# Block-recurrent attention with an ELU feed-forward: the states' result stored by quarters, the last quarter on two queues

## The chip, the cores and the metric

The kernel runs on one core of a Trainium2 chip. The metric is the device time of one execution in microseconds (us). Times given for a kernel are medians of several executions; the profile is one execution of its own, with a span from its first to its last instruction that is a little shorter than the measured time.

The engines are called as the profile calls them: PE is TensorE (matmuls; PEld is its weight load), DVE is VectorE, ACT is ScalarE, POOL is GpSimd, SP is SyncE. SPq and ACTq are the instruction queues of SP and ACT, where DMAs are issued.

## The reference, cut to what matters

```python
# x: (8, 8, 512, 64), state: (8, 8, 32, 64), w_in: (512, 2048), w_out: (2048, 512), all float32
scores = scale * x @ state.T                 # tokens read the states
xread = softmax(scores) @ state
scores2 = scale * state @ x.T                # states read the tokens
sread = softmax(scores2) @ x
y = concat([xread, sread], axis=2)           # per batch 512 token rows and 32 state rows
y = y.transpose(0, 2, 1, 3).reshape(8 * 544, 512)
h = y @ w_in
g = where(h > 0, h, exp(min(h, 0)) - 1)      # ELU
out = g @ w_out                              # (4352, 512)
```

Each of the 8 batches has 544 rows in the output: 512 for its tokens and, behind them, 32 for its states.

## The kernel before, in words

The work goes batch by batch. The first batch (`first_batch`) also loads and converts the weights, in an order that a written plan sets out. Batches 1 to 7 (`batch`) each compute the feed-forward of their 512 token rows and, woven in between, the attention of the next batch. The state rows of all batches, 8 x 32 = 256 of them, are kept in `read` and are computed together at the very end, in `states()` (lines 685 to 694), which runs once after the last batch.

`states()` first makes the hidden layer for the 256 rows, 128 features at a time (`ffn1_state`, with ACT and DVE making the ELU into `g_all`). Then it multiplies by `w_out` with one object of the class `Strassen` (lines 438 to 518). This is a scheme of Strassen's kind: the 256 x 512 result is cut into two halves of rows, h = 0 and 1, and two halves of columns, q = 0 and 1, and comes out of seven products where plain blocks would need eight. One product is 16 weight loads and 16 matmuls of 128 x 256 (`product`); the products accumulate in two PSUM banks, and after each of them one quarter of the result is copied or added into the SBUF tile `o_sb`, of 128 partitions x 2 (h) x 512 columns. `sums` makes the sums of blocks that the products take.

`steps()` returns the seven products in the order in which they run. `copy(ps, h, q)` is an ACT copy into quarter (h, q); `add(ps, h, q)` is a DVE addition onto what stands there:

```python
def p1(): ...; self.copy(bank_a, 0, 0)     # n = 0
def p2(): ...; self.add(bank_b, 0, 0)      # n = 1, and a DVE update of a12
def p6(): ...; self.copy(bank_a, 1, 0)     # n = 2
def p7(): ...; self.copy(bank_b, 1, 1)     # n = 3
def p5(): ...; self.add(bank_a, 1, 1)      # n = 4
def p4(): ...; self.add(bank_b, 1, 0)      # n = 5
def p3(): ...; self.copy(bank_a, 0, 1)     # n = 6
return [p1, p2, p6, p7, p5, p4, p3]
```

In a batch (line 683) the tile goes out in one DMA (`store`). In `states()` each batch's 32 rows lie elsewhere in the output, so there are eight DMAs, all on SP's queue, after the last step. Batch b's rows are the 32 partitions from (b mod 4) x 32, in half b // 4 of the tile.

What sets the order: PE and SP keep the order of the program throughout. ACT, DVE and POOL keep it in the first batch only; from batch 1 on (lines 698 and 699) the framework orders their instructions. The framework also makes every wait between engines and DMAs, from what each instruction reads and writes. `g_all`, `o_sb` and the weights are each one tile of which instructions use slices. The sequence at the program's end, that waits for all DMAs and brings the engines together, stands under line 728 in the profile.

Nearly all instructions carry line 94 in the profile, that of a helper, so groups are told apart by the tiles that they write and read. `out_dram<-o_sb` is a store of the result.

Of the kernel before, what the change touches and what calls it, by code (L numbers as in the profile page):

```python
# [25 lines left out]
def kernel(  # L26
# [15 lines left out]
    B, H, S, D = x.shape  # L42
    NS = state.shape[2]
    DM, DF = moe_w_in.shape
    P = 128
# [5 lines left out]
    SB = S + NS  # L51
# [8 lines left out]
    out_b = out.rearrange("(b s) c -> b s c", b=B)  # L60
# [27 lines left out]
    class InOrder:  # L88
# [10 lines left out]
    tensor, sync, vector, scalar, gpsimd = (  # L99
        InOrder(e) for e in (nc.tensor, nc.sync, nc.vector, nc.scalar, nc.gpsimd)  # L100
    )
# [292 lines left out]
    def ffn1_state(fo):  # L394

        ps = bank(3 + (fo + 1) % 3)[:, : B * NS]
        for co in range(NP):
            matmul(
                ps,
                w_in[:, fo // 2, co, fo % 2 * P : (fo % 2 + 1) * P],  # L400
                st["xT"][:, co].rearrange("p b s -> p (b s)"),
                start=(co == 0),
                stop=(co == NP - 1),
            )
        elu(ps, fo)
# [279 lines left out]
    def states():  # L685
        for fo in range(FO):
            ffn1_state(fo)
        half = Strassen(0)
        half.sums()
        for f in half.steps():  # L690
            f()
        for b in range(B):
            c, i = divmod(b, P // NS)
            sync.dma_start(out=out_b[b, S:SB], in_=half.o_sb[i * NS : (i + 1) * NS, c])

    first_batch()
    load_x(2, [sync])
# [2 lines left out]
    for b in range(1, B):  # L700
        batch(b)
    states()


# [28 lines left out]
```

## Time and profile before

| What | Value |
|---|---|
| Time, median of three executions | 774.3 us (773.92 to 775.31) |
| Span of the profiled execution | 773.4 us |
| The same execution as measured | 775.13 us |
| Mean granted clock of TensorE | 0.994 |
| Stores `out_dram<-o_sb` of 512 KB (token rows) | 16, on SPq |
| Stores `out_dram<-o_sb` of 64 KB (state rows) | 8, on SPq |
| Start of the first and the last of these eight | 767.6 and 770.8 us |

A line of a timeline or of a group names the engine, the line, the operation, the tiles (written <- read), the shapes and the number of instructions; "128x256 f32" is partitions x elements. In brackets stands how long the engine was idle before, and what ended that. A DMA's issuing instruction is short; when its data has landed is told apart, as the time from issue to landing.

### The profile page before, as it was taken

To read this page: it belongs to the slowest core of one execution; us is meant where nothing else is said; L and a number is where in the kernel's file an instruction comes from. 1 tells how busy PE (TensorE), PEld (TensorE's weight loads), DVE (VectorE), ACT (ScalarE), POOL (GpSimd) and SP (SyncE) were. 2 spreads that over 40 slices of the span, in tenths; PEclk is the share of its full clock that TensorE was granted. 3 is DMA by queue.
4 is the path that set the end of the run, shared out by engine and by line. 5 is a ranking of instruction groups with operands and counts; after the bars stand their busy time and mean duration, and the time that the engine had idled before them with its cause. 6 is when DMAs were issued, how large, how long until landed. Compare 5 with 4: busy or idle time off the path is not lost.

```text
span 773.4 us, 9742 instructions
## 1 busy us (share of the span) xinstructions
PE 744.9 (96%) x4016; PEld 499.8 (65%) x4016; DVE 351.7 (45%) x590; ACT 315.5 (41%) x585; POOL 35.1 (5%) x38
## 2 busy tenths in 40 slices
PE   3599999999999999999999999999999999999996
PEld 1234444468845786478846885578647884688885
DVE  2999979473135611481047413571148114601230
ACT  4799874642056213641164304630264106400420
POOL 0200002002000200010000200020001100000000
PEclk9899999999999999999999999999999999999999
DMA  9555400700030003000030003000000000000001
GB/s 283 217 200 198 108 1 28 137 1 22 7 83 1 1 28 81 1 1 28 28 56 1 2 27 82 1 1 28 27 1 1 28 4 24 1 28 1 27 1 27
DMA packets 44844, 35.22 MB, mean 46 GB/s; under 512 B 36352, under 2 KB 36352, under 8 KB 44800
## 3 DMA queue, kind: packets, MB, share of 16 engines
q1 hardware_dynamic: 41632, 33.82, 15.1%
q10 hardware_dynamic: 3168, 0.79, 0.5%
q8 instruction: 31, 0.51, 0.3%
q14 instruction: 13, 0.11, 0.0%
HBM read 25.69 MB, written 8.91 MB: 45 GB/s over the span
## 4 chain that ended last, share of the span: by engine, by line
PE 95%; DVE 2%; DMA 1%; ACT 1%; issue 0%; ACTq 0%; DVEq 0%
PE ps L94 95%; DMA x_sb<-in_x_dram 1%; DVE w_in L94 1%; DMA s_sb<-in_state_dram 0%; ACT raw L94 0%; DVE total_t L94 0%; ACT xT L94 0%; DVE top L94 0%; ACT e_sb L94 0%; DVE aT L94 0%; DVE t_sb L94 0%; DVE top_t L94 0%; ACT w_in L94 0%; ACT m_sb L94 0%; DVE total L94 0%
## 5 line engine op out<-in xcount | busy, mean ns | idle before, releaser
L94 PE MATMUL ps<-w_out,g_all 128*128 128x256 f32 (+1 forms) x1088 | 273.7, 406 | 0.0
L94 PEld LDWEIGHTS ps<-w_out,g_all 128*128 128x128 f32 x1088 | 205.2, 190 | 58.5 <-issue 31.3
L94 PE MATMUL ps<-aT,m_sb 128*128 128x512 f32 x512 | 228.2, 600 | 4.3 <-DVE aT L94 3.3
L94 PEld LDWEIGHTS ps<-aT,m_sb 128*128 128x128 f32 x512 | 96.9, 192 | 126.7 <-issue 119.5
L94 DVE SCALAR_TENSOR_TENSOR g_all<-e_sb,ps 128x512 f32<-128x512 f32 (+1 forms) x144 | 94.6, 658 | 169.6 <-ACT e_sb L94 169.6
L94 ACT ACTIVATE e_sb<-ps 128x512 f32<-128x512 f32 (+1 forms) x144 | 82.4, 572 | 96.0 <-PE ps L94 78.3
L94 ACT COPY o_sb<-ps 128x256 f32<-128x256 f32 (+1 forms) x62 | 23.4, 378 | 237.1 <-PE ps L94 237.1
L94 DVE TENSOR_TENSOR o_sb<-o_sb,ps 128x256 f32<-128x256 f32 x45 | 19.0, 421 | 208.6 <-PE ps L94 206.1
L94 PE MATMUL ps<-t_w,s 128*128 128x256 f32 x480 | 109.2, 381 | 0.0
L94 PEld LDWEIGHTS ps<-t_w,s 128*128 128x128 f32 x480 | 90.6, 190 | 17.1 <-issue 5.0
L94 ACT ACTIVATE e_sb<-e_sb 128x512 f32<-128x512 f32 (+1 forms) x144 | 87.2, 606 | 4.5
L94 PE MATMUL ps<-t_w,g_all 128*128 128x256 f32 x240 | 54.3, 379 | 0.0
L94 PEld LDWEIGHTS ps<-t_w,g_all 128*128 128x128 f32 x240 | 45.1, 190 | 5.9
L94 ACT ACTIVATE raw<-raw 128x512 f32<-128x512 uint32 x64 | 43.6, 681 | 1.0
L94 POOL TENSOR_TENSOR t_sb<-t_sb,top_t 128x512 f32<-128x512 f32 x16 | 17.6, 1108 | 542.1 <-DVE top_t L94 542.1
L94 PE MATMUL ps<-w_in,kT 64*32 64x512 f32 (+1 forms) x576 | 33.6, 554 | 0.0
L94 PE MATMUL ps<-xT_state,w_in 128*128 128x256 f32 x128 | 27.8, 379 | 0.0
L94 PEld LDWEIGHTS ps<-xT_state,w_in 128*128 128x128 f32 x128 | 24.3, 190 | 3.3
L94 ACT COPY m_sb<-ps 128x512 f32<-128x512 f32 x24 | 13.6, 581 | 29.2 <-PE ps L94 29.2
L94 DVE COPY m_sb<-ps 128x512 f32<-128x512 f32 x40 | 25.5, 681 | 0.0
L94 PEld LDWEIGHTS ps<-w_in,kT 64*32 64x32 f32 x576 | 9.3, 107 | 23.3 <-issue 19.4
L94 ACT COPY xT<-ps 128x512 f32<-128x512 f32 x32 | 16.6, 596 | 5.3 <-PE ps L94 5.3
(54 smaller groups left out, 379.6 us busy)
## 6 DMA issues: line engine op xcount, KB each, us to landing
raw<-in_moe_w_in_dram SPq DMA_DIRECT2D x16, 512.0 KB, 5.5
raw<-in_moe_w_out_dram SPq DMA_DIRECT2D x16, 512.0 KB, 3.3
out_dram<-o_sb SPq DMA_DIRECT2D x16, 512.0 KB, 2.7
x_sb<-in_x_dram SPq DMA_DIRECT2D x30, 256.0 KB, 5.0
x_sb<-in_x_dram ACTq DMA_DIRECT2D x2, 256.0 KB, 6.1
out_dram<-o_sb SPq DMA_DIRECT2D x8, 64.0 KB, 1.7
s_sb<-in_state_dram ACTq DMA_DIRECT2D x4, 64.0 KB, 2.9
s_sb<-in_state_dram SPq DMA_DIRECT2D x4, 64.0 KB, 2.6
```

The lines of the kernel that those rows point to most:

```text
L94: ins = getattr(self.engine, name)(*args, **kw)
```

## The change

In `states()`, the loop over the eight batches behind the last step goes. In its place, four of the seven steps are followed by four DMAs each, one for each group of 32 partitions, that store the quarter which this step completes: after n = 1 quarter (0, 0), after n = 4 quarter (1, 1), after n = 5 quarter (1, 0), after n = 6 quarter (0, 1). Each DMA moves 32 rows x 256 columns, 32 KB in pieces of 1 KB, where it was 32 rows x 512 columns, 64 KB in pieces of 2 KB. There are 16 DMAs instead of 8, with the same bytes in total. Twelve are on SP's queue; of the last four, two are on SP's and two on ACT's, by turns.

```diff
@@ -687,11 +687,21 @@
             ffn1_state(fo)
         half = Strassen(0)
         half.sums()
-        for f in half.steps():
+        for n, f in enumerate(half.steps()):
             f()
-        for b in range(B):
-            c, i = divmod(b, P // NS)
-            sync.dma_start(out=out_b[b, S:SB], in_=half.o_sb[i * NS : (i + 1) * NS, c])
+            quarter = {1: (0, 0), 4: (1, 1), 5: (1, 0), 6: (0, 1)}.get(n)
+            if quarter is None:
+                continue
+            c, q = quarter
+            cols = slice(q * DM // 2, (q + 1) * DM // 2)
+            for i in range(P // NS):
+                engine = scalar if n == 6 and i % 2 else sync
+                engine.dma_start(
+                    out=out_b[c * P // NS + i, S:SB, cols],
+                    in_=half.o_sb[i * NS : (i + 1) * NS, c, cols],
+                )
```

Here `c` is the half of rows h and `P // NS` is 4.

## The prediction

> **What bounds the kernel now.** I read the engine shares and the chain of waits first. TensorE is busy for 96% of the span, and the chain that ends last is TensorE for 95%. So anything that does not lie on TensorE's time, or after its last matmul, is hidden.
>
> ```profile
> PE 744.9 (96%) x4016; PEld 499.8 (65%) x4016; DVE 351.7 (45%) x590; ACT 315.5 (41%) x585; POOL 35.1 (5%) x38
> ...
> PE 95%; DVE 2%; DMA 1%; ACT 1%; issue 0%; ACTq 0%; DVEq 0%
> ```
>
> The change touches only the last stage, so the next view is the timeline of its end: start, length, engine, operation.
>
> ```profile
> 749.74 3.62 PE L94 MATMUL ps<-t_w,s 128*128 128x256 f32 x16
> 749.99 0.42 DVE L94 TENSOR_TENSOR o_sb<-o_sb,ps 128x256 f32<-128x256 f32 x1 [2.02 <-issue]
> ...
> 760.37 0.42 DVE L94 TENSOR_TENSOR o_sb<-o_sb,ps 128x256 f32<-128x256 f32 x1 [8.82 <-PE ps L94]
> ...
> 763.75 0.42 DVE L94 TENSOR_TENSOR o_sb<-o_sb,ps 128x256 f32<-128x256 f32 x1 [2.96 <-PE ps L94]
> ...
> 767.20 0.37 ACT L94 COPY o_sb<-ps 128x256 f32<-128x256 f32 x1 [9.99 <-PE ps L94]
> 767.60 3.63 SPq L94 DMA_DIRECT2D out_dram<-o_sb  x8
> ```
>
> The four writes shown complete the four quarters of the result buffer: (0,0) at 749.99 + 0.42 = 750.41, (1,1) at 760.79, (1,0) at 764.17, (0,1) at 767.57. All eight stores start after the last one, though three quarters have been ready for 3 to 17 us. The same stretch by the result buffer `o_sb` gives issue times (length min/median/max, first and last start) and the time from issue to landing:
>
> ```profile
> L94 SPq DMA_DIRECT2D out_dram<-o_sb x8: 344/420/432, 767.6 to 770.8; - x8
> ...
> DMA to landing us min/median/max: 1.6/1.7/1.7
> ```
>
> The eight starts are (770.8 - 767.6) / 7 = 0.46 us apart; one landing takes 1.7 us, hardly more for the last than for the first. So the queue's issuing rate sets the end, not the bandwidth. The table of stretches confirms it; its columns are the stretch, its length, five engines' busy time, the TensorE clock, the DMA share and GB/s:
>
> ```profile
> 767.57:770.81 3.24, 0.00 (x0) 0.00 (x0) 0.00 (x0) 0.01 (x1) 0.00 (x0) 1.00 0.41 104
> 770.81:772.52 1.71, 0.00 (x0) 0.00 (x0) 0.00 (x0) 0.00 (x0) 0.00 (x0) 0.51 0.43 110
> 772.52:773.35 0.83, 0.00 (x0) 0.00 (x0) 0.00 (x0) 0.00 (x0) 0.00 (x0) 0.50 0.00 0
> ```
>
> The tail after the last copy is 3.24 us of issuing, 1.71 us for the last landing, 0.83 us of the program's end: 5.78 us in which no engine computes, at some 104 GB/s. By source line, the end (line 728) is seven semaphore steps of SP and short drains.
>
> **What the Trainium skill says.** (1) "DMA: Bandwidth & Descriptors", section "Issuing engines are not separate DMA queues": DMAs from SP and ACT run on the same 16 DMA engines, and a second issuer saves only the sequencer's issue time. Issue time is just what this tail consists of (3.24 of 5.78 us), and the share of 0.41 says the DMA engines have room. (2) Same page, "Anatomy of one DMA": about 2.0 us fixed, mostly the write's receipt, and bytes / 436 GB/s on top; given for GpSimd's path. The trace has 1.7 us for 64 KB on SP's queue, which I use. By the page's slope, an estimate, 32 KB less saves 0.08 us: halving a store doesn't halve its landing. (3) Same page, "Rules for kernel authors": below 64 KB a transfer is mostly overhead. The change makes 16 stores of 32 KB of 8 of 64 KB; what matters is where the overhead lies.
>
> **The change part by part.** *Three quarters stored early (12 stores on SP).* Each quarter's four stores take 4 x 0.46 = 1.84 us of SP's queue. (0,0) would be issued from 750.4 to 752.3, (1,1) from 760.8 to 762.6, (1,0) from 764.2 to 766.0. The nearest gap to the next quarter is 764.17 - 760.79 = 3.4 us, so SP is idle again before each, and 1.6 us before the last at 767.57. SP keeps program order and has nothing else left: batch 7 issues no loads, and its last whole-tile store (line 683) comes ahead of this stage. Last landing of (1,0): about 764.2 + 1.4 + 1.7 = 767.3. Cost 0, hidden beside TensorE's products.
>
> Could these transfers slow the products? I compared a stretch that holds a 512 KB store with one that doesn't:
>
> ```profile
> 715.50:718.50 3.00, 3.00 (x16) 2.64 (x15) 0.42 (x1) 1.07 (x3) 0.00 (x0) 1.00 0.43 175
> ...
> 752.00:755.00 3.00, 3.00 (x16) 2.64 (x15) 0.00 (x0) 0.37 (x1) 0.00 (x0) 1.00 0.00 0
> ```
>
> Sixteen matmuls in 3.00 us either way: 0.
>
> *The last quarter, four stores on two queues.* Two on SP, two on ACT. SP: starts at 767.60 and 768.06. ACT has issued no DMA since the start of the program, so its price comes from there, where both queues loaded the states together:
>
> ```profile
> L94 ACTq DMA_DIRECT2D s_sb<-in_state_dram x4: 421/470/477, 0.7 to 2.2; - x4
> L94 SPq DMA_DIRECT2D s_sb<-in_state_dram x4: 374/440/451, 0.7 to 2.1; - x4
> ```
>
> Over the same 1.5 us each queue issued four, so they issue beside one another, ACT at 0.47 us. ACT's first store waits for its own copy, ended 767.57. The nearest row for that wait is ACT's drain in the end code, which starts at 767.2 and lasts up to 401 ns, thus to 767.61: 0.04 us after the copy. Hence ACT's stores start at about 767.61 and 768.10. Behind them on ACT stand only the drains of the end code, which wait for SP's side anyway, so no work is held up by ACT's issuing.
>
> *Landing of the last one.* 768.10 + 1.7 = 769.80. From below: half the bytes, -0.08 us (the skill's slope). From above: at the start, eight loads in flight from both queues took 2.2 to 3.2 us, median 2.8, in 256-byte pieces from HBM; 1.1 us over the 1.7. Here two stores of 32 KB start together, the 64 KB per 0.46 us that SP alone moves now, in pieces of 1 KB. I take 1.7.
>
> *The end.* The same 0.83 us; twice as many stores, but they are long landed. Bounds: 0 to 0.1 us for some more semaphore steps of 28 ns.
>
> Sum: 769.80 + 0.83 = 770.63 against 773.35, a gain of 2.72 us, made up of the issuing that goes from 3.24 to 0.53 us. The three other runs give 773.92 to 775.31, median 774.3, that is 0.9 us above this span (the profiled execution itself was measured at 775.13). The same gain from the median gives 774.3 - 2.7 = 771.6 us, -0.35%. A measurement of this kernel tells about 0.2%, 1.55 us, from no change; the gain is 1.75 times that.
>
> **The rivals.** *A, the forecast:* 771.6 us; with 0.7 us for the scatter of the runs, 770.9 to 772.3. Chance 0.76.
>
> *B, the buffer is guarded as a whole:* each write of a quarter waits until earlier stores have landed. (1,1): fourth store at 760.8 + 1.4, landed 763.9, so the add at 763.75 moves by 0.15; then (1,0) lands at about 767.4, and the last copy moves from 767.20 to 767.4. Some 0.2 us lost: 771.8. Against it: `g_all`, one tile, is written and read slice by slice without TensorE waiting. Chance 0.06.
>
> *C, the second queue brings little:* either ACT's stores land as late as the states' loads did (2.8 us: 770.9 + 0.83, gain 1.6), or the two queues take turns at issuing (fourth start at 767.6 + 3 x 0.46 = 769.0, end 771.5, gain 1.8). For it: ACT's queue is long idle, and a store on it isn't in the trace. Against: the side-by-side issues above. 772.5 to 772.7. Chance 0.13.
>
> *D, slower:* stores on different queues to the same output are ordered, each waiting for the landing of the one before, as SP and ACT alternate. The place is the last quarter: three handovers at 1.7 us put the last issue at 767.6 + 5.1 = 772.7, its landing at 774.4, the end at 775.2, +1.9 us: 776.2. It decides against the change from 3.2 / 3 = 1.07 us per handover. For it: before, all stores share one queue, so that ordering between queues was never seen. Against: the eight stores of one tensor don't wait for each other there, and their rows are disjoint. Chance 0.05.
>
> **How the numbers follow.** Faster by over 0.2% (below 772.75): nearly all of A (0.74), B (0.06), half of C (0.07): 0.87. Within: the rest of A and of C, 0.08. Slower: D, 0.05. The range takes A with its scatter and 0.1 us for a shorter landing, and reaches over C: 770.7 to 773.0, leaving out D and the scatter beyond C.
>
> **What would show it.** The timeline should have four groups of four stores, starting at 750.4, 760.8, 764.2 and 767.6, the last as two on SPq and two on ACTq, with 1.6 to 1.7 us to landing; SP's last start at 768.1 instead of 770.8; the span about 770.6. TensorE's products must keep their step of 3.45 us (749.74, 753.19, 756.64). B shows as an idle time of DVE or ACT before `o_sb` that ends on a DMA, C as a landing of over 2.5 us or starts 0.46 us apart across both queues, D as ACT's or SP's queue waiting for `out_dram`. The forecast is wrong if the last copy ends later than 767.6 by anything but scatter, or if the end takes over 1 us.

## The result, and the profile after

The changed kernel takes 771.95 us (median of 6 executions, 771.51 to 773.09) where the kernel before takes 774.7 us (median of 6, 773.84 to 775.34). The ratio is 0.9968 with a 95% interval of 0.9955 to 0.9981. That is 2.5 us less by the ratio and 2.75 us less by the medians; the forecast was 2.7 us. The profiled execution of the changed kernel spans 770.2 us, against 773.4 us.

First the timeline of the changed kernel's end, for the same instructions as before:

```profile
749.58 0.42 DVE L94 TENSOR_TENSOR o_sb<-o_sb,ps 128x256 f32<-128x256 f32 x1 [2.02 <-issue]
...
750.02 17.94 SPq L94 DMA_DIRECT2D out_dram<-o_sb  x14
...
759.95 0.42 DVE L94 TENSOR_TENSOR o_sb<-o_sb,ps 128x256 f32<-128x256 f32 x1 [8.81 <-PE ps L94]
...
763.33 0.42 DVE L94 TENSOR_TENSOR o_sb<-o_sb,ps 128x256 f32<-128x256 f32 x1 [2.96 <-PE ps L94]
766.78 0.37 ACT L94 COPY o_sb<-ps 128x256 f32<-128x256 f32 x1 [9.99 <-PE ps L94]
767.19 0.85 ACTq L94 DMA_DIRECT2D out_dram<-o_sb  x2
```

The first store now starts at 750.02, as soon as the first quarter is complete, and of the four that follow the last copy two are on ACT's queue. (The view merges SP's 14 stores into one line. Narrower timelines at 760.40 and 763.78 show the first stores of the second and the third quarter:)

```profile
760.40 0.31 SPq L94 DMA_DIRECT2D out_dram<-o_sb  x1
...
763.78 0.32 SPq L94 DMA_DIRECT2D out_dram<-o_sb  x1
```

The idle times in front of the writes of `o_sb` are what they were, and all end on TensorE or on issue: no write waits for a store. From the first write shown to the last it takes 17.20 us (749.58 to 766.78), before the change 17.21 us (749.99 to 767.20), so the early stores cost the products nothing. The last stores by the result buffer, with their time to landing:

```profile
L94 SPq DMA_DIRECT2D out_dram<-o_sb x2: 317/369/421, 767.2 to 767.5; - x2
L94 ACTq DMA_DIRECT2D out_dram<-o_sb x2: 378/406/434, 767.2 to 767.6; - x2
...
DMA to landing us min/median/max: 1.5/1.6/1.7
```

The last start of a store comes 0.45 us after the copy's end instead of 3.24 us after it. Cut at the same events as before (end of the last copy, start of the last store, its landing, end of the span), the tail is:

```profile
767.16:767.61 0.45, 0.00 (x0) 0.00 (x0) 0.00 (x0) 0.00 (x0) 0.00 (x0) 1.00 0.00 0
767.61:769.30 1.69, 0.00 (x0) 0.00 (x0) 0.00 (x0) 0.00 (x0) 0.00 (x0) 1.00 0.31 78
769.30:770.19 0.89, 0.00 (x0) 0.00 (x0) 0.00 (x0) 0.00 (x0) 0.00 (x0) 1.00 0.00 0
```

| Piece of the tail, us | Before | Forecast | After |
|---|---|---|---|
| Copy's end to last store's start | 3.24 | 0.53 | 0.45 |
| Last store's start to its landing | 1.71 | 1.70 | 1.69 |
| Landing to the end | 0.83 | 0.83 | 0.89 |
| Sum | 5.78 | 3.06 | 3.03 |

The tail accounts for 2.75 us. The two profiled spans differ by 3.2 us; the other 0.42 us are there before the tail begins, since the last copy starts at 766.78 instead of 767.20. Whether the change brings them too is the first question for the experiments.

### The profile page after: what moved, and what is told of

Its sections match the earlier page's. It is cut to its first block, busy times and chain, and to the rows that moved or that the text cites. A ratio compares the mean times of both kernels' runs of the same rounds, so it can differ in the third digit from the quotient of the medians.

```text
span 770.2 us, 9753 instructions
## 1 busy us (share of the span) xinstructions
PE 745.8 (97%) x4016; PEld 500.5 (65%) x4016; DVE 351.7 (46%) x590; ACT 315.7 (41%) x585; POOL 35.2 (5%) x38
## 4 chain that ended last, share of the span: by engine, by line
PE 95%; DMA 2%; ACT 1%; DVE 1%; issue 0%; ACTq 0%
PE ps L94 95%; DMA x_sb<-in_x_dram 1%; DMA raw<-in_moe_w_out_dram 1%; DVE w_in L94 1%; ACT raw L94 1%; DMA s_sb<-in_state_dram 0%; DVE total_t L94 0%; ACT xT L94 0%; ACT w_in L94 0%; ACT e_sb L94 0%; DVE aT L94 0%; ACT m_sb L94 0%; DVE total L94 0%; ACTq L94 0%; ACT o_sb L94 0%
```

## The experiments

The theory: the tail is the issuing of the stores that are left when the last copy ends, at some 0.46 us each on a queue, plus one landing and the program's end, both fixed. Its rivals: the bytes set the tail, one of the two parts of the change does nothing, the second queue is dear, or the change also gains ahead of the tail. Below, "tail" is always the time from the end of the last copy to the end of the span. Each version has one trace, the changed kernel two. The times alone tell the versions that are faster than the kernel before from it, but mostly not from each other, so the comparison between versions rests on the tails in their traces.

### The changed kernel once more

No edit. Is the 0.42 us ahead of the tail part of the gain?

> The changed kernel itself once more, to see which part of its gain stays. Theory (the gain is the issuing time that leaves the tail): from the end of the last copy to the end of the span 3.0 us where the kernel before has 5.8 us; the last copy itself ends between 766.9 and 767.8 us, anywhere in that band, since the 0.42 us by which it came earlier in the first trace came from the loads at the start. Rival (the change also gains 0.4 us ahead of the tail): the last copy ends at 767.15 us or earlier again, and the ratio of times stays at or below 0.9963. Theory's ratio: 0.9965.

Measured: 772.24 us against 774.88 us, ratio 0.9965 (0.9953 to 0.9977).

```profile
767.04 0.37 ACT L94 COPY o_sb<-ps 128x256 f32<-128x256 f32 x1 [9.99 <-PE ps L94]
767.44 0.78 SPq L94 DMA_DIRECT2D out_dram<-o_sb  x2
767.44 0.85 ACTq L94 DMA_DIRECT2D out_dram<-o_sb  x2
```

The copy ends at 767.41, neither as early as in the first trace (767.16) nor as late as before the change (767.57); the tail is 3.03 us again. The end of that copy wanders from 766.47 to 768.12 us over the profiled executions of this study, though the code up to there computes the same. So the 0.42 us are within what one execution differs from the next, and no gain of the change is shown by them. The ratio is the theory's 0.9965; its interval does not exclude the rival's 0.9963, so it is the traces that speak here. In the first pair of traces most of the difference is there within 12 us: TensorE's waits for the loads of `x_sb` come to 2.2 us in the kernel before and to 1.8 us in the changed one.

### The early quarters alone

```diff
-                engine = scalar if n == 6 and i % 2 else sync
+                engine = sync
```

> The quarters stored early, but all 16 stores on SP's queue. Theory (issuing on one queue at 0.46 us is the price): the last quarter's four starts lie 0, 0.40, 0.86 and 1.33 us after the first, the tail after the last copy is 0.03 + 1.33 + 1.6 + 0.85 = 3.8 us, so the gain is 2.0 us of 774.5, ratio 0.9974. Rival (the second queue brings nothing of its own, the early quarters are all): tail of 3.0 us as in the changed kernel, ratio 0.9965.

Measured: 772.53 us, ratio 0.9976 (0.9967 to 0.9985).

```profile
766.10 0.37 ACT L94 COPY o_sb<-ps 128x256 f32<-128x256 f32 x1 [9.99 <-PE ps L94]
766.50 1.71 SPq L94 DMA_DIRECT2D out_dram<-o_sb  x4
```

Four issues take 1.71 us from first start to last end, where two queues took 0.85 us. The tail is 3.70 us, where 3.8 was expected, with landings of 1.5 to 1.6 us. So the early quarters bring 5.78 - 3.70 = 2.08 us, and the second queue 3.70 - 3.03 = 0.67 us more. The intervals of the two ratios overlap; the 0.67 us rest on the traces' tails, not on the times.

### The second queue alone

```diff
-            sync.dma_start(out=out_b[b, S:SB], in_=half.o_sb[i * NS : (i + 1) * NS, c])
+            (sync, scalar)[b % 2].dma_start(out=out_b[b, S:SB], in_=half.o_sb[i * NS : (i + 1) * NS, c])
```

(on the kernel before)

> The other part alone: the kernel before with its eight 64 KB stores behind the last step, by turns on SP and ACT. Theory (both queues issue side by side, nothing is limited by bytes): four starts on each queue up to 1.4 us after the first, landing 1.7 us, tail 0.03 + 1.4 + 1.7 + 0.85 = 4.0 us, gain 1.8 us, ratio 0.9977. Rival (the transfers themselves limit the end once two queues feed them): landings grow to 2.3 us or more, tail 4.6 us, ratio 0.9985.

Measured: 772.79 us, ratio 0.9977 (0.9968 to 0.9986), as the theory had it; the tail is 3.89 us.

```profile
763.71 0.84 ACTq L94 DMA_DIRECT2D out_dram<-o_sb  x2
766.71 0.37 ACT L94 COPY o_sb<-ps 128x256 f32<-128x256 f32 x1 [9.99 <-PE ps L94]
767.11 1.74 SPq L94 DMA_DIRECT2D out_dram<-o_sb  x4
767.11 0.85 ACTq L94 DMA_DIRECT2D out_dram<-o_sb  x2
```

One thing went otherwise than expected. Two of ACT's four stores start at 763.71, ahead of the last copy. ACT isn't held to the program's order in this stage, and the two batches on ACT's queue that lie in half 1 have their 512 columns complete once (1,0) is. SP, which is held to it, still issues four behind the copy, so the end is still set by four issues in a row, and the number fits for that reason. The landings, 1.7 to 2.1 us, are somewhat longer where four stores of 64 KB start within 0.4 us (2.0 and 2.1 us for ACT's two), yet the one that ends the program took 1.7 us: the rival's 2.3 us isn't seen.

Each part alone brings about 2 us (2.08 and 1.89 us by the tails), together they bring 2.75 us. They shorten the same thing, the row of issues behind the copy, from eight to four, and together to two.

### Twice as many stores, the same bytes

```diff
-            sync.dma_start(out=out_b[b, S:SB], in_=half.o_sb[i * NS : (i + 1) * NS, c])
+            for q in range(2):
+                cols = slice(q * DM // 2, (q + 1) * DM // 2)
+                sync.dma_start(
+                    out=out_b[b, S:SB, cols], in_=half.o_sb[i * NS : (i + 1) * NS, c, cols]
+                )
```

(on the kernel before)

> The kernel before with the same bytes cut into sixteen stores of 32 KB, all on SP's queue behind the last step. Theory (the number of issues sets the tail): fifteen steps of 0.46 us, 6.9 us of issuing, tail 0.03 + 6.9 + 1.6 + 0.85 = 9.4 us, 3.6 us more than before, ratio 1.0047. Rival (the bytes set it): tail of 5.8 us, ratio 1.000.

Measured: 777.52 us, ratio 1.0037 (1.0025 to 1.0049), 2.6 us slower by the medians.

```profile
766.77 0.37 ACT L94 COPY o_sb<-ps 128x256 f32<-128x256 f32 x1 [9.99 <-PE ps L94]
767.17 6.81 SPq L94 DMA_DIRECT2D out_dram<-o_sb  x15
```

The tail is 8.80 us, where 9.4 was expected. Fifteen stores stand behind the copy, not sixteen: the first in SP's order is of quarter (0,0), which had long been complete, and it went out at 750.01 us. The sum of the expectation had one step of 0.46 us too many. Fifteen issues take 6.81 us, 0.45 us each, though each moves half the bytes. That excludes the bytes as the limit: halving a store doesn't make its issue cheaper, and the same output in twice as many pieces behind the copy costs 3.0 us.

### The early quarters in twice as many stores

```diff
-            cols = slice(q * DM // 2, (q + 1) * DM // 2)
-            for i in range(P // NS):
+            pieces = 1 if n == 6 else 2
+            width = DM // 2 // pieces
+            for i in range(P // NS):
+                for k in range(pieces):
+                    cols = slice(q * DM // 2 + k * width, q * DM // 2 + (k + 1) * width)
```

> The changed kernel with each early quarter stored by eight pieces of 16 KB instead of four of 32 KB; the last quarter as it is. Theory (early issuing is hidden as long as SP's queue is empty when the last copy ends): the doubled stores of quarters (0,0) and (1,1) cost nothing; those of (1,0) take 8 x 0.46 = 3.7 us from 3.4 us before the last copy's end, so SP's first store of the last quarter starts 0.24 us after the copy instead of 0.03 us, and the tail is 3.2 us instead of 3.0 us; TensorE keeps its 3.45 us per product; ratio 0.9967. Rival (the stores disturb the products or the adds, by traffic or by waits on the buffer): products above 3.5 us, or waits of ACT or DVE on a DMA before they write the result buffer, and over 0.5 us lost ahead of the last copy.

Measured: 772.99 us, ratio 0.9976 (0.9966 to 0.9987). The tail is 3.70 us, 0.67 us more than with four stores per quarter, where 0.2 us was expected. Is it the products? One product per line, two with heavy stores and one without:

```profile
749.78:753.23 3.45, 3.45 (x18) 3.04 (x17) 1.56 (x2) 0.00 (x0) 0.00 (x0) 1.00 0.08 19
...
756.68:760.13 3.45, 3.45 (x18) 3.04 (x17) 0.00 (x0) 0.37 (x1) 0.00 (x0) 1.00 0.00 0
...
763.58:767.03 3.45, 3.45 (x18) 3.04 (x17) 0.42 (x1) 0.00 (x0) 0.00 (x0) 1.00 0.14 33
```

They keep their count: a stretch of 3.45 us holds or touches 18 matmuls in each. The first write of the timeline starts at 750.35 and the last copy at 767.56, 17.21 us apart as in the kernel before, and the waits of this stretch show no DMA ahead of a write. So the rival is out. The tail in the same three pieces:

```profile
767.93:768.96 1.03, 0.00 (x0) 0.00 (x0) 0.00 (x0) 0.00 (x1) 0.00 (x0) 1.00 0.18 43
768.96:770.52 1.56, 0.00 (x0) 0.00 (x0) 0.00 (x0) 0.00 (x0) 0.00 (x0) 1.00 0.34 88
770.52:771.63 1.11, 0.00 (x0) 0.00 (x0) 0.00 (x0) 0.00 (x0) 0.00 (x0) 1.00 0.00 0
```

The last store starts 0.58 us later than in the changed kernel (1.03 against 0.45 us), its landing is 0.13 us shorter, and the end is 0.22 us longer (1.11 against 0.89 us). What starts late is SP's queue. By the result buffer from 764.75 us (first fence) and from 768.5 us on (second):

```profile
L94 SPq DMA_DIRECT2D out_dram<-o_sb x8: 367/419/425, 764.8 to 768.0; - x8
```

```profile
L94 SPq DMA_DIRECT2D out_dram<-o_sb x2: 367/397/427, 768.5 to 769.0; - x2
```

Quarter (1,0) was complete at 764.53 us, but its first store starts at 764.83, because eight stores of (1,1) were still being issued: they take 8 x 0.46 = 3.7 us, and the two quarters are 3.4 us apart. The expectation overlooked this backlog. It passes on: the eight of (1,0) start up to 768.0, and SP's first store of the last quarter starts at 768.55, 0.62 us after the copy's end at 767.93, while ACT's start at 767.96 as planned. The mechanism of the theory holds, its sum missed this link. Early stores are free only while their issuing fits in between the quarters.

The sum missed the longer end too. SP waits for the DMAs' semaphores one after another, and those that it hasn't checked when the last store lands follow then. These are its semaphore steps right after the last landing, in the kernel before, the changed one and this one:

```profile
L728 SPq EVENT_SEMAPHORE  x1: 28/28/28, 772.5 to 772.5; - x1
...
L738 SPq EVENT_SEMAPHORE  x2: 28/28/28, 769.3 to 769.4; - x2
...
L741 SPq EVENT_SEMAPHORE  x5: 28/28/28, 770.5 to 770.8; - x5
```

One step goes with an end of 0.83 us, two with 0.89, five with 1.1: some 0.06 to 0.07 us for each step more. So the program's end isn't quite fixed, as the theory took it to be.

### The last quarter on ACT alone

```diff
-                engine = scalar if n == 6 and i % 2 else sync
+                engine = scalar if n == 6 else sync
```

> The last quarter's four stores all on ACT's queue, early quarters on SP as in the changed kernel. Theory (either queue issues at the same price, and only sharing the four between two queues saves anything): four starts over 1.3 to 1.4 us, tail 3.7 to 3.9 us, as with all four on SP. Rival (ACT's queue, long idle, is dearer): a first start over 0.1 us after the copy, steps of over 0.5 us, or landings of over 2 us.

Measured in one execution, 773.68 us, which is too few for a ratio. The tail is 3.79 us, with landings of 1.5 to 1.6 us.

```profile
767.75 0.37 ACT L94 COPY o_sb<-ps 128x256 f32<-128x256 f32 x1 [9.99 <-PE ps L94]
768.15 1.79 ACTq L94 DMA_DIRECT2D out_dram<-o_sb  x4
```

The first store starts 0.03 us after ACT's own copy, and four take 1.79 us, against 1.71 us on SP. An ACT queue that issued no DMA for over 760 us is 0.08 us dearer over four stores; the rival is out. The last store's landing, with all four on SP (first line) and with all four on ACT (second), is the same:

```profile
767.78:769.34 1.56, 0.00 (x0) 0.00 (x0) 0.00 (x0) 0.00 (x0) 0.00 (x0) 0.83 0.23 61
...
769.50:771.07 1.57, 0.00 (x0) 0.00 (x0) 0.00 (x0) 0.00 (x0) 0.00 (x0) 1.00 0.23 60
```

In the changed kernel, where both queues issue side by side, ACT's last store took 1.69 us.

### A third queue for the last quarter

```diff
-                engine = scalar if n == 6 and i % 2 else sync
+                engine = (sync, scalar, gpsimd, sync)[i] if n == 6 else sync
```

> The last quarter on three queues: two stores on SP, one on ACT, one on POOL. Theory (only the queue with most issues sets the tail): SP still issues two, so the last landing is SP's, at 0.03 + 0.36 + 1.58 = 1.97 us after the copy, where ACT's second landed at 2.14 us; tail 2.85 us if POOL's store lands within 1.9 us of the copy. Rival (POOL's queue is slower to start and to land): its store lands later than 2.1 us after the copy, and the tail is 3.0 us or more. Ratio 0.9964 in either case, told apart by the landings.

Measured: 772.4 us, ratio 0.9969 (0.9958 to 0.9981).

```profile
766.99 0.37 ACT L94 COPY o_sb<-ps 128x256 f32<-128x256 f32 x1 [9.99 <-PE ps L94]
767.38 0.78 SPq L94 DMA_DIRECT2D out_dram<-o_sb  x2
767.39 0.38 ACTq L94 DMA_DIRECT2D out_dram<-o_sb  x1
767.65 0.66 POOL L94 DMA_DIRECT2D out_dram<-o_sb  x1 [165.11 <-ACT o_sb L94]
```

POOL's store starts 0.3 us after the copy and lands 1.9 us later, at 2.17 us after the copy, so it is the last; SP's second landed at 1.95 us, close to the theory's 1.97 us. The tail is 3.16 us, 0.13 us more than with two queues. Only 0.03 us of that is the landing, since ACT's second store landed at 2.14 us in the changed kernel; the rest is the end, 0.99 us instead of 0.89. The rival was right: a store on POOL lands no sooner than a second one on ACT, so nothing is gained.

### The last copy by two engines

```diff
-                    self.copy(bank_a, 0, 1)
+                    part, w = self.part(0, 1), DM // 4
+                    scalar.copy(out=part[:, :w], in_=bank_a[:, :w])
+                    vector.tensor_copy(out=part[:, w:], in_=bank_a[:, w : 2 * w])
```

(in `states()` alone)

> The changed kernel with the last copy shared: ACT copies one half of its columns, DVE the other. Theory (the tail starts when the last copy ends, and every us ahead of the stores counts in full): two copies of 128 x 128 of some 0.27 us side by side in place of one of 0.37 us, so the first store starts 0.1 us earlier after TensorE's last product; end of the span 0.1 us earlier counted from there, 0.01% of the time, not to be seen in the ratio (0.9964). Rival (the two copies of one PSUM bank take turns, or the stores' second wait costs as much): the first store starts as late as in the changed kernel or later.

Measured: 772.32 us, ratio 0.9965 (0.9953 to 0.9978): no different from the changed kernel.

```profile
766.03 0.27 ACT L94 COPY o_sb<-ps 128x128 f32<-128x128 f32 x1 [9.99 <-PE ps L94]
766.33 0.29 DVE L94 COPY o_sb<-ps 128x128 f32<-128x128 f32 x1 [3.33 <-ACT o_sb L94]
766.64 0.78 SPq L94 DMA_DIRECT2D out_dram<-o_sb  x2
```

The copies run one after the other: DVE's idle time ends on ACT's. From the start of ACT's copy to the first store it now takes 0.61 us, where the changed kernel takes 0.40 us. The rival was right. Why DVE waits, whether for the bank of PSUM or for the tile `o_sb`, wasn't tried. Against the tile speaks that writes of one quarter of it never waited for the stores from another.

No version tried beats the changed kernel. In this last one the tail is 3.02 us, but counted from the later of two copies; from the start of ACT's copy to the end of the span it takes 3.61 us, the changed kernel 3.40 us.

## Why the prediction was right

The forecast was case A, 771.6 us, and 771.95 us was measured, within 770.9 to 772.3. By its steps:

- **What bounds the tail.** The prediction read from the eight starts 0.46 us apart that issuing sets the end, not bandwidth. Cutting the bytes per store in half left the issue at 0.45 us and made the tail 3.0 us longer; shown.
- **Three quarters early, at no cost.** Products at 3.45 us, no write held up, starts at 750.02, 760.40, 763.78; shown. The margin was put at 1.6 us of SP's queue before the last copy. With doubled stores SP came 0.6 us too late, so the margin is real; measured in the changed kernel, it is 1.7 us (the last early store starts at 765.1, its issue ends at 765.5, the copy at 767.16).
- **Two queues for the last quarter.** Forecast 0.53 us to the last start, measured 0.45 us: SP's first step was 0.36 us, not 0.46, and ACT's 0.42, not 0.49 (the prediction read 0.47 us for ACT, but its two starts, 767.61 and 768.10, lie 0.49 apart). The first step of a row is shorter than the mean of eight that was used. ACT's wait for its own copy, taken from a drain at 0.04 us, was 0.03 us.
- **The landing.** 1.7 us was taken, between 1.6 and 2.8. Measured 1.69 us for the store that lands last (1.5 to 1.7 over the four). That this fits to 0.01 us is in part luck, for two things that the prediction didn't take in cancel. Half the bytes on one queue land in 1.56 us instead of 1.71, which saves 0.15 us where the prediction estimated 0.08 from the skill's slope and left it out of its sum; and with two queues side by side ACT's last store takes 0.12 us longer than with ACT alone (1.69 against 1.57). Half the bytes shorten a landing little, which agrees with what "DMA: Bandwidth & Descriptors" of the Trainium skill says in "Anatomy of one DMA" for GpSimd's path, that a fixed part dominates at such sizes. The 1.1 us dearer landing, taken over from the states' loads, didn't come.
- **The end.** 0.89 us instead of 0.83, one semaphore step of SP more after the last landing; the allowance of 0.1 us covers it.
- **The time.** By the medians and by the tails the gain is 2.75 us, within 0.1 us of the forecast; by the ratio it is 2.5 us, with 1.5 to 3.5 us left open by the interval. The tail came within 0.03 us because 0.08 us too much for the issuing and 0.06 us too little for the end offset each other. The 0.35 us by which 771.6 is too low come from the base: six executions of the kernel before have a median of 774.7, not 774.3 us.

Of the rivals, B (the buffer guarded as a whole) is out by the idle times ahead of the writes, C (a second queue of little use) by the starts side by side and by 3.70 against 3.03 us of tail, D (queues waiting for one another's stores) by SP's and ACT's second starts 0.06 us apart, long before any landing.

One thing the prediction left unsaid: the gain isn't a sum over the two parts. Each alone brings about 2 us, and once one is made the other adds only 0.7 to 0.9 us.

## What to carry to other kernels

At the end of a kernel look at what stands between the last compute instruction and the end, and count issues, not bytes: eight small stores on one queue cost 0.46 us each, whatever their size here (16 to 64 KB), plus one landing of 1.5 to 1.7 us. Store each part of a result when it is complete, so that only the last part's issues are left, and share these between SP and ACT. Don't cut early stores so fine that the queue is still issuing them when the last part is ready: a backlog is passed from part to part and comes out at the end.

## What the runs showed that was not expected

- On a queue that isn't held to the program's order, the framework can put a store ahead: with stores by turns on SP and ACT at the very end, two of ACT's four went out 3.4 us before the last's data were there.
- A store from POOL started 0.3 us after the copy that it waits for, where SP and ACT needed 0.03 us, and landed 1.9 us after its start.
- ACT's and DVE's copies of two halves of one PSUM bank into one tile ran one after the other; why stays open.
- The program's end took 0.83 to 1.1 us after the last landing, longer where SP had more semaphores left to check.
- With the same computation ahead of it, the last copy ended anywhere from 766.47 to 768.12 us over the nine profiled executions that leave this copy whole. A difference of 1.6 us or less between two single spans says nothing by itself; the tail, counted from that copy, repeated within 0.01 us (3.03 us in both executions of the changed kernel).
